# Channel attention with a folded feed-forward layer: v's second tile is loaded and transposed earlier

## The chip, the cores and the metric

The kernel runs on one core of a Trainium2 chip. A core has TensorE (PE in the profile; its weight loads are listed as PEld), VectorE (DVE), ScalarE (ACT), GpSimd (POOL) and SyncE (SP), which each run their own instructions in order and wait for one another by semaphores. Sixteen DMA engines move data between device memory and SBUF (on-chip memory with 128 partitions), and within SBUF; TensorE writes its results to PSUM banks, from which VectorE and ScalarE copy them. The metric is the time of one execution on the device, in microseconds (us); less is better.

## The reference

The inputs are q, k and v of 4 x 6080 x 256, two weights, w_in (256 x 2048) and w_out (2048 x 256), and three scalars. All is float32.

```
qn = q / (norm(q, axis=1) + 1e-6);  kn = k / (norm(k, axis=1) + 1e-6)   # norms over the 6080 rows
s  = kn^T @ qn / tau                  # 256 x 256 for each batch
a  = softmax(s, last axis)
x  = (v @ a) as 24320 rows of 256
h  = x @ w_in;  r = max(h, 0);  g = s * r * r + b
out = g @ w_out
```

## The kernel before

**Algebra.** Since x = v a and h = x w_in, the kernel multiplies a by w_in first, once for each batch. The result (`wa`, 256 x 2048, held as two halves of 128 partitions by 2048 columns) is called the folded weight, and h is then v wa. The softmax's division is done as a scaling of the rows of the folded weight by `rs`, the reciprocal of the sums of the exponentials.

**Start, batch 0.** q and k come in 13 chunks of up to 512 rows, nearly all by DMAs that POOL issues and that convert from float32 to float16 on the way (the first three tiles come as float32 from SP's and ScalarE's queues). For each chunk TensorE adds to the Gram matrix `s_ps` (line 154), while ScalarE and VectorE form squares for the norms. The last chunks' k tiles are loaded before their q tiles. Between the chunks' matmuls `keep_busy` (line 551) issues filler matmuls, whose results nobody reads: one after each of the chunks 8, 7 and 6 from the end, two after the chunks 5 and 4 from the end (`FILL`, line 549). When the norms are summed, ScalarE makes the inverse norms of k and then of q (line 277, four steps each), VectorE scales the Gram matrix (line 302), and ScalarE takes the exponentials in two halves, `eT` (line 308).

**First block.** `first_block` (line 340) makes the first 256 columns of the folded weight. For each half of the exponentials it issues two matmuls for the row sums `r_ps` (line 347) and two for the product with w_in (line 352). VectorE then takes the reciprocal (line 356), and the two halves are scaled out of PSUM in pieces of 128 columns, one half by ScalarE (line 329), the other by VectorE (line 331). Before this block TensorE transposes v's first tile (`transpose_v`, line 463: eight transposes of 128 x 128 into one PSUM bank, then one VectorE copy of 128 x 1024), and one more filler is issued (line 595).

**Main loop.** The 24320 rows go in 48 groups of 512 (the last is of 256), and each group in 16 steps of 128 columns of the hidden layer, so step s is group s // 16, column block s % 16. In each step `mm1` (line 761) makes h for one column block; ScalarE and VectorE apply relu and square; then products with w_out follow, for most groups by a scheme of seven products of half size (line 932). The remaining blocks of batch 0's folded weight (`fold_one`, line 361) are issued at steps 0, 0, 1, 1, 3, 3, 5, 5, 8, 8 right after `mm1`: first columns 256 to 512, then 512 to 768, 768 to 1024, 1024 to 1536, 1536 to 2048.

**What sets the order.** The order on every engine is the order of the calls in the program (`po` keeps it). `at_step` puts side work at fixed steps: the transposes of v's second tile at step 12 (line 692), while from the third tile on v is transposed by DMAs from SP's queue (`crossbar_v`). POOL issues its DMAs in this order: q and k, v tile 0, the five pieces of w_in (256, 256, 512, 512 and 512 columns), v tile 1, four pieces of w_out, v tile 2, two scalars.

**Buffers.** PSUM has one Gram bank (`ps_gram`), two h tiles of two banks (`ps_h`) and three banks for everything else (`ps_o`), which each new tile takes in turn. `first_block` takes its two products from one o bank and one h tile, its row sums from an o bank; `bank` (line 442) gives that. v has four SBUF buffers for tiles as loaded and three for transposed ones.

Of the kernel before, what the change touches and what calls it, by code (L numbers as in the profile page):

```python
# [9 lines left out]
FP32 = mybir.dt.float32  # L10
# [6 lines left out]
def kernel(  # L17
# [12 lines left out]
    nc = tc.nc  # L30
    P = 128

    B, N, C = q.shape
# [11 lines left out]
    CH = C // P  # L45
    FT = Dff // P
# [8 lines left out]
    def po(ins):  # L55

        tc.keep_in_program_order(ins)
        return ins

    def pool(name, bufs, **kw):  # L60
        return ctx.enter_context(tc.tile_pool(name=name, bufs=bufs, **kw))
# [19 lines left out]
    ps_gram = pool("ps_gram", 1, space=PSUM)  # L81
# [9 lines left out]
    def h_tile(name):  # L91
        return ps_h.tile([P, 2, TG], FP32, tag="h_ps", name=name)
# [19 lines left out]
    class Gram:  # L112
# [147 lines left out]
        def finish_ops(self):  # L260
# [3 lines left out]
            def inverse(a=None):  # L264

                n = C + CH if a is None else (CH, C)[a]

                def part(i):
                    if i == 0:
                        st["r", a] = sm_pool.tile([P, n], FP32, tag=f"r{a}", name=f"r{a}")  # L270
                        if a is None:
                            st["r", 1], st["r", 0] = st["r", a][:, :C], st["r", a][:, C:]
                    r = st["r", a]
                    func, kw = [(AF.Ln, dict(bias=tiny)), (AF.Exp, dict(scale=0.5)),
                                (AF.Ln, dict(bias=eps)), (AF.Exp, dict(scale=-1.0))][i]
                    sums = self.n_all if a is None else self.n_ps[a]
                    po(nc.scalar.activation(out=r, in_=r if i else sums, func=func, **kw))  # L277
                    if i == 3 and a != 1 and inv_tau != 1.0:
                        po(nc.vector.tensor_scalar_mul(
                            out=st["r", 0], in0=st["r", 0], scalar1=inv_tau))  # L280

                return [lambda i=i: part(i) for i in range(4)]

            def norms(a):
                return lambda: self.add_norms(a, last=True)
# [19 lines left out]
            def exps(j):  # L305
                if j == 0:
                    st["e"] = sm_pool.tile([P, CH, C], FP16, tag="eT", name="eT")
                po(nc.scalar.activation(  # L308
                    out=st["e"][:, j, :], in_=st["t"][:, j], func=AF.Exp,
                    scale=st["r", 0][:, j : j + 1]))  # L310
                if j == 0:
                    self.wa = apool.tile([P, CH, Dff], FP16, tag="wa16", name="wa16")
# [12 lines left out]
            def scaled(f0, n, m, wa_ps):  # L325
                dst = self.wa[:, m, ds(f0, n)]
                third = self.b == 0 and f0 == 2 * NW
                if m == third and not (self.b == 0 and NW <= f0 < 2 * NW):
                    po(nc.scalar.mul(out=dst, in_=wa_ps, mul=st["rs"][:, m : m + 1]))  # L329
                else:  # L330
                    po(nc.vector.tensor_scalar_mul(
                        out=dst, in0=wa_ps, scalar1=st["rs"][:, m : m + 1]))
# [4 lines left out]
                                        w_in16[:, j, ds(f0, n)],  # L337
                                        start=(j == 0), stop=(j == CH - 1)))

            def first_block(n):  # L340

                two = [self.bank("wa_ps", CH, C)[:, 0, :n], h_tile("wa_ps")[:, 0, :n]]
                r_ps = self.bank("r_ps", CH, C)[:, :, 0]
                for j in range(CH):
                    exps(j)
                    for ch in range(CH):
                        po(nc.tensor.matmul(r_ps[:, ch : ch + 1], st["e"][:, j, ts(ch, P)],
                                            parts16, start=(ch == 0 and j == 0),
                                            stop=(ch == CH - 1 and j == CH - 1),
                                            skip_group_check=True))  # L350
                    for m in range(CH):
                        po(nc.tensor.matmul(two[m], st["e"][:, j, ts(m, P)],
                                            w_in16[:, j, :n],
                                            start=(j == 0), stop=(j == CH - 1)))
                st["rs"] = sm_pool.tile([P, CH], FP32, tag="rs", name="rs")
                po(nc.vector.reciprocal(out=st["rs"], in_=r_ps))
                for f0 in range(0, n, P):
                    for m in range(CH):
                        scaled(f0, P, m, two[m][:, ds(f0, P)])

            def fold_one(f0, n, m):
                def f():
                    wa_ps = self.bank("wa_ps", CH, C).rearrange("p a c -> p (a c)")[:, :n]
                    fold_mm(f0, n, m, wa_ps)
                    if self.b == 0 and f0 == 2 * NW and m == 1:
                        return at_step(5, lambda: scaled(f0, n, m, wa_ps))
                    scaled(f0, n, m, wa_ps)
                return f
# [60 lines left out]
            if self.b == 0:  # L429
                blocks = [(2 * P, 2 * P), (4 * P, 2 * P), (6 * P, 2 * P), (2 * NW, NW), (3 * NW, NW)]  # L430
                folds = [fold_one(f0, n, m) for f0, n in blocks for m in range(CH)]
                return [norms(1), *inverse(1), norms(0), *inverse(0), lambda: scale(CH),
                        lambda: first_block(2 * P)] + folds

            def sums_and_halves():
                sums()
# [12 lines left out]
    def group(g):  # L449
        t0 = g * TG  # L450
        return t0, min(TG, NT - t0) // P
# [3 lines left out]
    def load_v(g):  # L455
        t0, nj = group(g)
        v16 = vpool.tile([P, TG // P, C], FP16, tag="v16", name="v16")
        po(nc.gpsimd.dma_start(  # L458
            out=v16[:, :nj, :],
            in_=v_flat[t0 : t0 + nj * P, :].rearrange("(p j) c -> p j c", j=nj)))  # L460
        v_tiles[g] = v16

    def transpose_v(g):
        _, nj = group(g)
        v16 = v_tiles.pop(g)
        vT_ps = ps_o.tile([P, CH, TG], FP16, tag="o_ps", name="vT_ps")
        for j in range(nj):
            for ch in range(CH):
                po(nc.tensor.transpose(vT_ps[:, ch, ts(j, P)], v16[:, j, ts(ch, P)], ident16))  # L469
        vT = vtpool.tile([P, CH, TG], FP16, tag="vT", name="vT")  # L470
        po(nc.vector.tensor_copy(out=vT[:, :, : nj * P], in_=vT_ps[:, :, : nj * P]))
        vT_tiles[g] = vT

    def crossbar_v(g):

        _, nj = group(g)
        v16 = v_tiles.pop(g)
        vT = vtpool.tile([P, CH, TG], FP16, tag="vT", name="vT")
        for j in range(nj):
            po(nc.sync.dma_start_transpose(out=vT[:, :, ts(j, P)], in_=v16[:, j, :]))  # L480
        vT_tiles[g] = vT
# [25 lines left out]
    for c in range(NDIRECT, len(g0.chunks) - NLATE):  # L507
        g0.load(c)
        if c == NDIRECT:
            po(nc.gpsimd.affine_select(  # L510
                out=ident16, in_=ones_id, compare_op=ALU.is_equal, fill=0.0, base=0,
# [8 lines left out]
    def load_w_in(f0, f1, co=None):  # L520
        cs = slice(0, CH) if co is None else slice(co, co + 1)
        po(nc.gpsimd.dma_start(out=w_in16[:, cs, f0:f1], in_=w_in_rows[:, cs, f0:f1]))

    load_v(0)
    load_w_in(0, 2 * P)
    load_w_in(2 * P, NW)
    load_w_in(NW, 2 * NW)
    load_w_in(2 * NW, 3 * NW)
    load_w_in(3 * NW, Dff)
    w_out_rows = moe_w_out.rearrange("(fo p) d -> p fo d", p=P)  # L530
    load_v(1)

    NPIECE = FT // 4
    w_pieces = []
# [11 lines left out]
    g0.start()  # L546
    NCH0 = len(g0.chunks)

    FILL = {-8: 1, -7: 1, -6: 1, -5: 2, -4: 2}

    def keep_busy(n):

        for _ in range(n):
            po(nc.tensor.matmul(h_tile("idle_ps")[:, 0, :], fill[:, :P], fill, start=True,
                                stop=True, skip_group_check=True))

    norms_k, *rest = g0.finish_ops()
    inverse_k, norms_q, inverse_q, scale_s, first_block, folds = (
        rest[:4], rest[4], rest[5:9], rest[9], rest[10], rest[11:])
    late = range(NCH0 - NLATE, NCH0)  # L560
    for c in range(NCH0 - NLATE):
        ops = g0.norm_ops(c)
        for j in range(g0.chunks[c][2]):
            g0.mm(c, j)
        keep_busy(FILL.get(c - NCH0, 0))
        if c == NCH0 - NLATE - 1:
# [25 lines left out]
    for f in (*inverse_q, scale_s):  # L592
        f()
    transpose_v(0)
    keep_busy(1)
    first_block()


    acc = opool.tile([P, 4, C], FP32, tag="o_sb", name="acc")
# [60 lines left out]
    def at_step(s, f):  # L660
        side.setdefault(int(s), []).append(f)
# [6 lines left out]
    for i, f in enumerate(folds):  # L668
        early.setdefault(FOLDS[i], []).append(f)
    at_step(14, lambda: po(nc.vector.tensor_scalar_mul(  # L670
        out=s_out, in0=s_bc, scalar1=1.0 / (LAM * LAM))))
# [15 lines left out]
    for g in range(NG):  # L687
        if g >= 3:
            at_step(max(g - 4, 0) * FT + 2, lambda g=g: load_v(g))
        if g >= 1:  # L690
            if g == 1:
                at_step(12, lambda g=g: transpose_v(g))
            else:
                at_step((g - 2) * FT + 6, lambda g=g: crossbar_v(g))
    LATER = {(1, 0): {1: 5, 2: 4, 3: 3}, (1, 1): {0: 6, 1: 3, 2: 3, 3: 4, 4: 4},
             (1, 2): {0: 4, 1: 1, 2: 2, 3: 2, 4: 2}, (1, 11): {2: 1, 3: 1}}
    for b in range(2, B):
# [3 lines left out]
    for b in range(1, B):  # L701
# [6 lines left out]
        n = NCH * JC  # L708
# [247 lines left out]
    for s in range(NS + FT):  # L956
        g, m = divmod(s, FT)
# [8 lines left out]
        if work:  # L966
            items, n = work[0]
# [61 lines left out]
```

## Time and profile before

| what | value |
| --- | --- |
| median of 3 runs | 714.37 us (714.33 to 714.67) |
| span of the profiled execution, first to last instruction | 712.9 us |
| time of the profiled execution outside its span | not listed |
| TensorE busy | 692.9 us, 97% |
| VectorE, ScalarE, GpSimd busy | 635.6, 547.5, 114.1 us |
| mean granted TensorE clock | 0.998 |
| time before the first TensorE matmul | 10.96 us |
| first L761 matmul (main loop begins) | 37.84 us |

The profile is of one execution. Times count from its first instruction, so the span leaves out what the device does before the first and after the last instruction; the median of the runs holds that too. In the tables of stretches the columns are the stretch in us from the span's start, its length, then for PE, PEld, DVE, ACT and POOL the busy time with the number of instructions, then the granted TensorE clock (1.00 is full speed), the DMA engines' share and the GB/s that they moved. In a timeline each line gives start, time, engine, line of the kernel, operation, output and input tiles, and the count where several follow one another; brackets hold the idle time before it and what ended that. TensorE's matmuls are pipelined, so the time of a group reaches beyond the start of the next. The lists of DMA issues give the size and the us from issue to landing. Some matmul records can be missing from a trace.

### The profile page before, as it was taken

What the parts mean: (1) busy time and instruction counts of PE and PEld (TensorE: products, weight loads), DVE (VectorE), ACT (ScalarE), POOL (GpSimd) and SP (SyncE); (2) the same over time, 40 slices, a digit from 0 to 9 for tenths busy, and PEclk for the clock granted to TensorE, in tenths of its full rate; (3) what the DMA queues carried; (4) which work ended last, traced back from release to release, by engine and by line L of the source; (5) the groups of instructions that cost most, each with busy time, mean ns of one, the idle gap of its engine ahead of it and who ended that gap; (6) DMA issues with size and microseconds to landing.
All of it is one profiled execution on the core that took longest, in us unless ns stands there. A gap on an engine that the chain in (4) does not pass through costs nothing.

```text
span 712.9 us, 17531 instructions
## 1 busy us (share of the span) xinstructions
PE 692.9 (97%) x7422; PEld 502.9 (71%) x7422; DVE 635.6 (89%) x906; ACT 547.5 (77%) x598; POOL 114.1 (16%) x192
## 2 busy tenths in 40 slices
PE   3699999999999999999999999999999999999998
PEld 2456777776677777777677777777768777777777
DVE  4889999999988989998999899998998888888886
ACT  5689877787777777778877777777876777777875
POOL 4533132201202222111010222111000000000000
PEclk9999999999999999999999999999999999999999
DMA  9999999566566878465761888737323333321202
GB/s 213 207 259 168 186 164 137 114 109 122 105 136 109 133 137 144 110 92 101 156 131 50 148 134 150 129 76 96 101 65 75 94 71 75 97 61 46 83 31 75
DMA packets 87854, 83.55 MB, mean 117 GB/s; under 512 B 56368, under 2 KB 62784, under 8 KB 87776
## 3 DMA queue, kind: packets, MB, share of 16 engines
q0 software_dynamic: 27136, 44.00, 38.9%
q1 hardware_dynamic: 60128, 37.45, 21.1%
q8 instruction: 58, 0.95, 0.6%
q10 hardware_dynamic: 512, 0.98, 0.4%
q14 instruction: 20, 0.16, 0.1%
HBM read 78.91 MB, written 24.90 MB: 146 GB/s over the span
## 4 chain that ended last, share of the span: by engine, by line
PE 95%; DMA 4%; ACT 1%; issue 0%; DVE 0%; ACTq 0%; POOLq 0%
PE h_ps L761 46%; PE o_ps L932 40%; PE s_ps L154 5%; DMA qk<-in_q_dram 2%; DMA qk<-in_k_dram 1%; PE wa_ps L394 1%; PE o_ps L836 1%; PE o_ps L808 0%; PE wa_ps L336 0%; ACT r L277 0%; PE n_ps L252 0%; ACT sq L185 0%; ACT eT L308 0%; PE vT_ps L469 0%; DVE half L229 0%
## 5 line engine op out<-in xcount | busy, mean ns | idle before, releaser
L771 ACT ACTIVATE r<-h_ps 128x1024 f16<-128x1024 f32 (+1 forms) x384 | 388.5, 1013 | 144.2 <-PE h_ps L761 140.6
L761 PE MATMUL h_ps<-vT,wa 128*128 128x512 f16 (+7 forms) x1632 | 452.1, 364 | 0.5 <-ACT wa L329 0.5
L932 PEld LDWEIGHTS <-S 128*128 128x128 f16 x2944 | 198.1, 98 | 84.3
L932 PEld LDWEIGHTS <-g 128*128 128x128 f16 x2208 | 155.0, 98 | 74.0
L784 DVE TENSOR_TENSOR g<-r 128x2048 f16<-128x2048 f16 (+2 forms) x150 | 174.4, 1163 | 10.1 <-ACT r L771 9.7
L932 PE MATMUL o_ps<-T,S 128*128 128x128 f16 x2208 | 183.1, 219 | 0.0
L761 PEld LDWEIGHTS <-wa 128*128 128x128 f16 x1632 | 136.6, 98 | 19.0 <-ACT wa L329 1.0
L932 PE MATMUL o_ps<-w_out,g 128*128 128x128 f16 x1472 | 134.2, 219 | 0.0
L782 ACT ACTIVATE g<-r 128x1024 f16<-128x1024 f16 (+1 forms) x97 | 100.3, 1034 | 0.2
L789 DVE SCALAR_TENSOR_TENSOR o_sb<-o_ps,s_out,u 128x256 f32<-128x256 f32 x138 | 66.2, 480 | 36.1 <-PE o_ps L932 34.5
L154 PE MATMUL s_ps<-qk 128*128 128x256 f16 (+1 forms) x384 | 71.0, 287 | 15.6 <-ACT qk L145 11.0
L458 POOL DMA_DIRECT2D v<-in_v_dram x48 | 31.4, 662 | 239.9 <-DMA vT<-v 192.7
L215 POOL DMA_DIRECT2D f<-f x33 | 28.8, 874 | 245.9 <-DVE f L199 197.3
L789 DVE SCALAR_TENSOR_TENSOR u<-o_ps,s_out,rowconst 128x256 f32<-128x256 f32 x138 | 65.7, 476 | 0.0
L932 PE MATMUL o_ps<-w_out,S 128*128 128x128 f16 x736 | 63.5, 219 | 0.0
L932 PE MATMUL o_ps<-N,g 128*128 128x128 f16 x736 | 63.4, 219 | 0.0
L185 ACT ACTIVATE sq<-qk 128x1024 f16<-128x1024 f16 (+2 forms) x53 | 54.5, 1041 | 4.5 <-DMA qk<-in_k_dram 1.9
L861 DVE TENSOR_TENSOR S<-S,g 128x2048 f16<-128x2048 f16 (+1 forms) x47 | 56.4, 1200 | 1.2
L859 DVE TENSOR_TENSOR S<-g 128x2048 f16<-128x2048 f16 (+1 forms) x47 | 56.0, 1192 | 0.0
L863 DVE TENSOR_TENSOR S<-g 128x2048 f16<-128x2048 f16 x46 | 55.8, 1214 | 0.0
L865 DVE TENSOR_TENSOR S<-g,S 128x2048 f16<-128x2048 f16 x46 | 55.8, 1213 | 0.0
L154 PEld LDWEIGHTS <-qk 128*128 128x128 f16 (+1 forms) x384 | 33.0, 103 | 21.2 <-ACT qk L145 11.0
(103 smaller groups left out, 334.4 us busy)
## 6 DMA issues: line engine op xcount, KB each, us to landing
out_dram<-o_sb SPq DMA_DIRECT2D x43, 512.0 KB, 3.0
v<-in_v_dram POOLq DMA_DIRECT2D x47, 256.0 KB, 5.0
qk<-in_q_dram POOLq DMA_DIRECT2D x43, 256.0 KB, 7.7
qk<-in_k_dram POOLq DMA_DIRECT2D x42, 256.0 KB, 6.4
f<-f POOLq DMA_DIRECT2D x30, 128.0 KB, 3.1
vT<-v SPq DMA_TRANSPOSE x182, 3.0
w<-in_moe_w_out_dram POOLq DMA_DIRECT2D x4, 512.0 KB, 9.9
out_dram<-o_sb SPq DMA_DIRECT2D x8, 256.0 KB, 4.1
```

The lines of the kernel that those rows point to most:

```text
L154: po(nc.tensor.matmul(self.s_ps[:, ch, :], qc[:np_, j, ts(ch, P)], kc[:np_, j, :], start=(c == 0 and j == 0 and ch == 0), stop=(c == len(s ...
L185: po(nc.scalar.activation(out=st["sq"][:np_, a, js, :], in_=(qc, kc)[a][:np_, js, :], func=AF.Square))
L761: po(nc.tensor.matmul(dst, wa[:, ci, ts(m, P)], src, start=(ci == 0), stop=(ci == CH - 1), skip_group_check=True))
L771: po(nc.scalar.activation(out=r16[:, :, i % 2, :n], in_=h_tiles.pop((g, i))[:, :, :n], func=AF.Relu))
L782: po(nc.scalar.activation(out=dst, in_=src, func=AF.Square))
L784: po(nc.vector.tensor_mul(dst, src, src))
L789: po(nc.vector.scalar_tensor_tensor(out=dst, in0=src, scalar=s_out, op0=ALU.mult, in1=add, op1=ALU.add))
L859: po(nc.vector.tensor_add(T[1], A21, A22))
L861: po(nc.vector.tensor_sub(T[2], T[1], A11))
L863: po(nc.vector.tensor_sub(T[3], A11, A21))
L865: po(nc.vector.tensor_sub(T[4], A12, T[2]))
L932: po(nc.tensor.matmul(st[name][:, j, :], a()[:, i, ts(j, P)], w[:, i, :], start=first, stop=last, skip_group_check=True))
```

## The change

Five things change.

- The DMA of v's second tile is issued right after that of the first, ahead of the five pieces of w_in.
- v's second tile is transposed on TensorE before the first block, where a filler stood; the transposes at step 12 go.
- Its copy out of PSUM is made in two halves (128 x 512 each). The first is issued on VectorE before the reciprocal, the second after the scalings of the first block.
- `first_block` takes its two products from the two banks of one h tile, and its row sums from the Gram bank.
- The fillers after the chunks 8, 7 and 6 from the end are left out; those after 5 and 4 stay.

```diff
-            def first_block(n):
-                two = [self.bank("wa_ps", CH, C)[:, 0, :n], h_tile("wa_ps")[:, 0, :n]]
-                r_ps = self.bank("r_ps", CH, C)[:, :, 0]
+            def first_block(n, between, after):
+                both = h_tile("wa_ps")
+                two = [both[:, m, :n] for m in range(CH)]
+                r_ps = ps_gram.tile([P, CH, C], FP32, tag="s_ps", name="r_ps")[:, :, 0]
                 for j in range(CH):
                     exps(j)
...
+                between()
                 st["rs"] = sm_pool.tile([P, CH], FP32, tag="rs", name="rs")
                 po(nc.vector.reciprocal(out=st["rs"], in_=r_ps))
                 for f0 in range(0, n, P):
                     for m in range(CH):
                         scaled(f0, P, m, two[m][:, ds(f0, P)])
+                after()
...
-                        lambda: first_block(2 * P)] + folds
+                        lambda *fs: first_block(2 * P, *fs)] + folds
...
-    def transpose_v(g):
+    def transpose_v(g, parts=1):
...
         vT = vtpool.tile([P, CH, TG], FP16, tag="vT", name="vT")
-        po(nc.vector.tensor_copy(out=vT[:, :, : nj * P], in_=vT_ps[:, :, : nj * P]))
         vT_tiles[g] = vT
+        def copy(part):
+            cs = slice(0, CH) if parts == 1 else slice(part, part + 1)
+            po(nc.vector.tensor_copy(out=vT[:, cs, : nj * P], in_=vT_ps[:, cs, : nj * P]))
+        if parts == 1:
+            return copy(0)
+        return [lambda i=i: copy(i) for i in range(parts)]
...
     load_v(0)
+    load_v(1)
     load_w_in(0, 2 * P)
     load_w_in(2 * P, NW)
     load_w_in(NW, 2 * NW)
     load_w_in(2 * NW, 3 * NW)
     load_w_in(3 * NW, Dff)
     w_out_rows = moe_w_out.rearrange("(fo p) d -> p fo d", p=P)
-    load_v(1)
...
-    FILL = {-8: 1, -7: 1, -6: 1, -5: 2, -4: 2}
+    FILL = {-5: 2, -4: 2}
...
     transpose_v(0)
-    keep_busy(1)
-    first_block()
+    first_block(*transpose_v(1, CH))
...
-        if g >= 1:
-            if g == 1:
-                at_step(12, lambda g=g: transpose_v(g))
-            else:
-                at_step((g - 2) * FT + 6, lambda g=g: crossbar_v(g))
+        if g >= 2:
+            at_step((g - 2) * FT + 6, lambda g=g: crossbar_v(g))
```

## The prediction

> **What bounds the kernel now.** I read the engines' totals and the chain that ended last, then TensorE's busy time by stretch, then the order of time between 28 and 42 us, which is where the change acts.
>
> ```profile
> PE 692.9 (97%) x7422; PEld 502.9 (71%) x7422; DVE 635.6 (89%) x906; ACT 547.5 (77%) x598; POOL 114.1 (16%) x192
> PE 95%; DMA 4%; ACT 1%; issue 0%; DVE 0%; ACTq 0%; POOLq 0%
> ```
>
> ```profile
> 38.00:100.00 62.00, 62.00 (x547) 42.48 (x546) 59.87 (x97) 54.25 (x64) 19.78 (x34) 1.00 1.04 200
> ```
>
> The second fence is the table by stretch (PE busy first, granted clock third from the end). TensorE is busy in all 62 of 62 us, at clock 1.00, and so in every later stretch up to 700. The end is therefore the start of the first L761 matmul, at 37.84 us, plus TensorE's work after it, plus any new hole. VectorE is busy 59.87 us there, but the waits of TensorE after 38 us list no VectorE. Before 31 us the transfers bind (205 GB/s, DMA share above 1), then a chain through ScalarE up to the exponentials.
>
> ```profile
> 35.39 0.62 PE L469 MATMUL vT_ps<-ident,v 128*128 128x128 f16 x8
> 35.82 0.47 PE L554 MATMUL idle_ps<-fill 128*128 128x512 f32 x1
> 36.52 0.20 PE L347 MATMUL r_ps<-parts,eT 128*128 128x1 f16 x2 [0.23 <-ACT eT L308]
> 36.58 0.38 PE L352 MATMUL wa_ps<-w_in,eT 128*128 128x256 f16 x2
> 36.92 0.20 PE L347 MATMUL r_ps<-parts,eT 128*128 128x1 f16 x2
> 36.98 0.38 PE L352 MATMUL wa_ps<-w_in,eT 128*128 128x256 f16 x2
> 37.84 0.60 PE L761 MATMUL h_ps<-vT,wa 128*128 128x512 f16 x2 [0.48 <-ACT wa L329]
> ...
> 35.38 0.45 PEld L469 LDWEIGHTS <-v 128*128 128x128 f16 x8 [0.39 <-DMA v<-in_v_dram]
> ```
>
> In TensorE's timeline the first tile of v is already waited for: it lands at 35.3 and its transposes start at 35.38. The first block starts at 36.52, held by the exponentials, and ends at 36.98 + 0.38 = 37.36. So there is about 1 us between the landing of v's first tile and the work that sets the end.
>
> ```profile
> 28.31 0.53 POOL L458 DMA_DIRECT2D v<-in_v_dram  x1 [0.80 <-DMA qk<-in_k_dram]
> 29.55 0.74 POOL L522 DMA_DIRECT2D w_in<-in_moe_w_in_dram  x1 [0.70 <-DMA qk<-in_q_dram]
> 30.75 2.13 POOL L522 DMA_DIRECT2D w_in<-in_moe_w_in_dram  x3 [0.47 <-DMA qk<-in_k_dram]
> 33.15 0.70 POOL L522 DMA_DIRECT2D w_in<-in_moe_w_in_dram  x1 [0.27 <-DMA qk<-in_q_dram]
> 33.85 0.57 POOL L458 DMA_DIRECT2D v<-in_v_dram  x1
> ```
>
> ```profile
> v<-in_v_dram POOLq DMA_DIRECT2D x1, 256.0 KB, 7.0
> ...
> w_in<-in_moe_w_in_dram POOLq DMA_DIRECT2D x1, 128.0 KB, 6.4
> ...
> w_in<-in_moe_w_in_dram POOLq DMA_DIRECT2D x1, 128.0 KB, 7.2
> ...
> w_in<-in_moe_w_in_dram POOLq DMA_DIRECT2D x1, 256.0 KB, 7.4
> ...
> q8 instruction: 1, 0.02, 2.0%
> ```
>
> POOL's issues in order of time, then those issues' times to landing, asked one by one. Issue plus time gives: v tile 0 at 28.31 + 7.0 = 35.31; w_in columns 0 to 256 at 29.55 + 6.4 = 35.95; columns 256 to 512 at 30.75 + 7.2 = 37.95; columns 512 to 1024 at about 31.46 + 7.4 = 38.86 (the group of three split evenly). The reader is to see that the queue is in order and full, so whatever is put in front delays everything behind it by its own transfer.
>
> **The change part by part.**
>
> *Second v tile ahead of w_in.* It is one issue of 0.53 us on POOL, moved past five of 0.70 to 0.74. Nothing moves on SP. POOL itself runs over 6 us ahead of the landings, so its order costs nothing; the transfers do. 256 KB at the 204 to 206 GB/s of these microseconds take 1.27 us. So v tile 1 lands at 35.31 + 1.27 = 36.58 and the five pieces of w_in 1.27 us later each: 37.22, 39.22, 40.13 and so on. What follows on POOL (w_out, v tile 2) keeps its place and date.
>
> *Transposes before the first block.* Eight transposes occupy TensorE for 0.45 us (the chain has them at 47.58 as "0.45 PE vT_ps L469 x8"). TensorE works in order: behind the landing at 36.58 they run from 36.65 to 37.10. Queued behind them are the row sums and the first block, which started at 36.52. The first block's products then wait for w_in, to 37.22. From there two products (0.22), two sums (0.06), two products (0.22) and the drain (about 0.16, the 0.38 of a pair less its 0.22) end at 37.88, against 37.36. Both exponentials are done by 36.9, so nothing else holds them. Delay: 0.52, call it 0.54 with the semaphore hop seen at 36.47 to 36.52. ScalarE, VectorE and the first L761 wait for this end; L761 goes from 37.84 to 38.38.
>
> *The next two pieces.* The first fold of columns 256 to 512 ran at 38.29; it would run at 38.83, but its w_in lands at 39.22: 0.41 more with the hop. Columns 512 to 1024 were wanted at 39.16, now at 39.16 + 0.95 = 40.11, and land at 40.13: nothing more. The pieces for 41.76 and 43.91 landed at 40.1 and 41.4 and stay ahead by 1 us and more. Delay in all: 0.95.
>
> *The copy out of PSUM in two halves.* One copy of 0.68 us at 48.06 goes, two of 128x512 come. The trace has none of that shape: the 0.68 of double the size bounds it from above and half of it, 0.34, from below; I take 0.41, as for the half-width additions just before. The first half stands ahead of the reciprocal on VectorE, from 37.27 to 37.68; the row sums end at about 37.64, so the reciprocal is held 0.04 (0 to 0.3 by the bounds) and ends at 37.86, still before the first block's product at 37.88. The second follows the scalings and fits before the next fold, where VectorE had 0.69 idle. The copy saved at 48 us hides already behind TensorE: 0.
>
> *Transposes gone from step 12.* 0.45 us off TensorE's solid stretch: a full gain of 0.45.
>
> *Three fillers at 20, 22.5 and 25 us, and the one at 35.82, left out.* Each was 0.47 us inside waits for q tiles (1.18, 1.27 and 1.18 us) and, the last, for the exponentials. Covered by those waits: 0 in time. What they did to the clock is the second rival.
>
> *PSUM places.* The first block takes one h tile in place of one and an o bank, the row sums the Gram's bank, free since the scaling at 36.14: 0.
>
> Sum: 0.54 + 0.41 - 0.45 = +0.50 us. Bounds: the second piece of w_in came 2.00 us after the first, where its 128 KB take 0.64 at 205 GB/s. The excess of 1.36 stands beside one packet of the instruction queue, which took 2.0% of 16 engines in a window of 3 us, 0.96 us of one engine. If it falls behind these pieces, 0.41 goes: +0.09. If it falls on v tile 1, that lands at 37.94, transposes end at 38.45 and the first block at 39.1, but w_in's 39.22 then costs nothing extra: +1.3. If on the first piece of w_in, landing at 38.58: 1.88 - 0.45 = +1.43. I take the middle because the packet comes with TensorE's program (at 35.89 it was near the filler), which the change lets wait at just that place until 36.6; it then meets the second piece as before.
>
> The sum is against the profiled execution, whose span is 712.9; no other time of that execution is listed. The median of the runs, 714.37, lies 1.5 us outside the span, which I carry over: 714.37 + 0.50 = 714.9.
>
> **The rivals.**
>
> *Hidden anyway.* If v and w_in land sooner than in order, only the transposes are left ahead of the block: they end at 37.10 or earlier, against 36.52 to 36.9, about 0.4, and the gain is 0.45. Time 714.2 to 714.4; at best, with no delay at all, 713.9. For it: w_in's first need is for two of its 16 column blocks only. Against: 99% busy transfers.
>
> *The clock drops.* This ends slower.
>
> ```profile
> 23.62:27.04 3.42, 1.56 (x12) 1.15 (x13) 3.18 (x8) 2.65 (x3) 1.59 (x4) 1.00 1.13 211
> 27.04:30.45 3.41, 3.38 (x16) 2.04 (x14) 2.15 (x5) 2.11 (x2) 1.75 (x3) 0.50 1.13 205
> 33.86:37.28 3.42, 3.09 (x44) 1.99 (x42) 2.06 (x6) 2.81 (x9) 2.68 (x4) 1.00 1.28 200
> ```
>
> After a stretch with 1.56 of 3.42 us busy the next had clock 0.50; after the full one it was 1.00 again. In 33.86 to 37.28 TensorE was busy 3.09; without the filler and with the wait for v it is about 1.42 + 0.62 + 0.62 = 2.66, above 1.56, so I take no drop: 0. If it drops at 37.28, the stretch up to 40.69 runs at half speed. The work that would be done in it, about 2.3 us of full rate, shrinks to about 1.4 because of the new waits: +0.9 on top of 0.5, 715.8. Where the drop falls on a solid stretch it costs 3.41 / 2 = 1.7: 716.6. It decides from the point where the busy time that counts falls to about 1.6 in such a stretch. The missing fillers before 26 us may bring a drop earlier, but the four that stay fill 27 to 31.4, where it came back.
>
> A rule speaks against the change here. The Trainium skill, "TensorE: Matmul & The Clock Gate", Part 4, says that transposes do not count as busy time for the clock as other matmuls do. By it the window would hold 1.42, under the 1.56 that lost the clock, and the sum would be +1.4 instead of +0.5; no row here tells, since in the one window with transposes other work was enough.
>
> *The instruction packet hits v or w_in's first piece.* +1.3 to +1.43, 715.7 to 715.8, as worked out above.
>
> **How the numbers follow.** Forecast (+0.1 to +1.0) 0.50; hidden anyway 0.12; clock 0.16; packet 0.15; something unseen 0.07. A measurement of this kernel can tell 0.2%, 1.43 us, from no change. So within 0.2%: 0.50 + 0.12, half of the packet's (0.08) and 0.02 of the clock's: 0.72. Slower: 0.14 + 0.07 + 0.04 = 0.25. Faster: 0.03, since TensorE has only 0.45 to give. Range: 714.1, below the forecast's low end of 714.46 and into the hidden case, to 716.2, between the clock's two prices; about 0.1 is left out at each end.
>
> **What would show it.** In the changed profile: v tile 1 landing near 36.6 with TensorE waiting for it; the first L352 waiting for w_in to about 37.2; the first L761 at 38.4 and not 37.84; a hole before the first L336 of up to 0.5; no transposes at 47.6; solid TensorE work after 41 with about 0.45 us less of it; clock 1.00 after 31. It is wrong if L761 starts by 38.0, if a stretch after 33.9 has clock 0.50, or if TensorE shows holes after 42.

## The result and the profile after

The changed kernel took 717.38 us (median of 5 runs, 716.74 to 718.43) against 714.40 us (714.33 to 715.45) for the kernel before. The ratio is 1.0043, with a 95% interval of 1.0032 to 1.0055: slower by 3.0 us. The forecast was 714.9, with 714.1 to 716.2 as its range.

The profiled execution's span went from 712.9 to 715.4 us. First the page's totals and the chain's window from 34 us, where each line gives start, length and what it was.

```profile
PE 693.1 (97%) x7418; PEld 502.3 (70%) x7418; DVE 635.8 (89%) x907; ACT 547.6 (77%) x598; POOL 114.6 (16%) x192
```

```profile
29.65 8.24 DMA v<-in_v_dram
37.89 0.05 issue
37.94 0.62 PE vT_ps L472 x8
...
39.55 0.38 ACT wa L329
39.93 0.04 issue
39.98 1.03 PE h_ps L767 x2
```

TensorE's busy time is the same, 693.1 us against 692.9, though four fillers are gone and the transposes only moved: part of the work ran slower. The chain no longer passes through the exponentials but through the transfer of v's second tile, which took 8.24 us from its issue and landed at 37.89 us. Now TensorE's timeline around the first block:

```profile
35.43 0.62 PE L472 MATMUL vT_ps<-ident,v 128*128 128x128 f16 x8
37.94 0.62 PE L472 MATMUL vT_ps<-ident,v 128*128 128x128 f16 x8 [1.89 <-DMA v<-in_v_dram]
38.40 0.19 PE L348 MATMUL r_ps<-parts,eT 128*128 128x1 f16 x2
38.45 0.59 PE L353 MATMUL wa_ps<-w_in,eT 128*128 128x256 f16 x2
38.83 0.24 PE L348 MATMUL r_ps<-parts,eT 128*128 128x1 f16 x2
38.93 0.59 PE L353 MATMUL wa_ps<-w_in,eT 128*128 128x256 f16 x2
39.98 1.03 PE L767 MATMUL h_ps<-vT,wa 128*128 128x512 f16 x2 [0.46 <-ACT wa L329]
40.80 1.06 PE L336 MATMUL wa_ps<-w_in,eT 128*128 128x256 f16 x4
41.66 0.71 PE L767 MATMUL h_ps<-vT,wa 128*128 128x512 f16 x2
42.20 0.60 PE L336 MATMUL wa_ps<-w_in,eT 128*128 128x256 f16 x4
```

TensorE stands 1.89 us for v. The first block's row sums start at 38.40 and not at 36.52. The pair of L353 takes 0.59 where it took 0.38, the main loop's first pair 1.03 where it took 0.60, the first four folds 1.06 against 0.60. Only at 42.20 are four folds back at 0.60. The table by stretch says why (length, busy times, and granted clock third from the end):

```profile
35.06:38.47 3.41, 1.50 (x23) 1.05 (x21) 1.35 (x3) 1.80 (x7) 1.22 (x3) 1.00 1.28 199
38.47:41.88 3.41, 2.95 (x17) 1.47 (x15) 1.63 (x5) 1.14 (x3) 2.85 (x5) 0.50 1.21 260
41.88:45.30 3.42, 3.42 (x21) 1.92 (x20) 3.16 (x7) 2.41 (x4) 1.34 (x3) 1.00 1.05 362
```

The stretch with the stand was busy 1.50 us, and the next ran at half clock. A third thing shows in the two engines that scale the first block, here ScalarE's and then VectorE's timeline:

```profile
39.55 0.37 ACT L329 ACTIVATE wa<-wa_ps,rs 128x128 f16<-128x128 f32 x1 [2.56 <-PE wa_ps L353]
40.34 0.37 ACT L329 ACTIVATE wa<-wa_ps,rs 128x128 f16<-128x128 f32 x1 [0.42 <-DVE wa L331]
```

```profile
39.95 0.35 DVE L331 TENSOR_SCALAR wa<-wa_ps,rs 128x128 f16<-128x128 f32 x1 [0.68 <-ACT wa L329]
40.74 0.35 DVE L331 TENSOR_SCALAR wa<-wa_ps,rs 128x128 f16<-128x128 f32 x1 [0.44 <-ACT wa L329]
```

Before, ScalarE did its two from 37.42 and VectorE its two from 37.44, side by side. Now each waits for the other, since both read one PSUM tile.

**Where the 2.6 us of the spans went.** The row sums start 1.88 us later. From there to the first main matmul it is 1.58 us against 1.32, 0.26 more. From there to the third and fourth of the early folds it is 2.22 (39.98 to 42.20) against 1.32, 0.90 more. Together 3.04; without the transposes at step 12, 0.45 less; so 2.59, and the spans differ by 2.60 (715.45 and 712.85 before rounding). The medians differ by 2.98; the 0.4 beyond the spans lies outside them and in the spread of the runs, and is not traced here.

A fourth thing costs nothing in this trace but matters below. POOL issues the sixth v tile's load at 50.49 us, where the kernel before did it at 59.47. Kernel before, then after:

```profile
49.95 0.53 POOL L137 DMA_DIRECT2D qk<-in_q_dram  x1 [0.27 <-DMA v<-in_v_dram]
59.47 0.53 POOL L458 DMA_DIRECT2D v<-in_v_dram  x1 [8.99 <-DVE g L784]
```

```profile
50.49 0.54 POOL L461 DMA_DIRECT2D v<-in_v_dram  x1
51.01 0.55 POOL L137 DMA_DIRECT2D qk<-in_k_dram  x1
51.53 0.56 POOL L137 DMA_DIRECT2D qk<-in_q_dram  x1
52.68 0.54 POOL L137 DMA_DIRECT2D qk<-in_k_dram  x1 [0.60 <-DMA v<-in_v_dram]
53.70 0.53 POOL L137 DMA_DIRECT2D qk<-in_q_dram  x1 [0.48 <-DMA qk<-in_k_dram]
```

### The profile page after: what moved, and what is told of

It reads as the page before. It is cut to its first block, busy times and chain, and to the rows that moved or that the text cites. A ratio compares the mean times of both kernels' runs of the same rounds, so it can differ in the third digit from the quotient of the medians.

```text
span 715.4 us, 17523 instructions
## 1 busy us (share of the span) xinstructions
PE 693.1 (97%) x7418; PEld 502.3 (70%) x7418; DVE 635.8 (89%) x907; ACT 547.6 (77%) x598; POOL 114.6 (16%) x192
## 3 DMA queue, kind: packets, MB, share of 16 engines
q0 software_dynamic: 27136, 44.00, 38.6%
## 4 chain that ended last, share of the span: by engine, by line
PE 94%; DMA 4%; POOL 1%; issue 0%; ACT 0%; DVE 0%; POOLq 0%
PE h_ps L767 46%; PE o_ps L938 40%; PE s_ps L154 4%; DMA qk<-in_k_dram 2%; DMA qk<-in_q_dram 1%; PE wa_ps L397 1%; DMA v<-in_v_dram 1%; PE o_ps L842 1%; POOL qk L137 1%; PE o_ps L814 0%; PE wa_ps L336 0%; PE wa_ps L353 0%; PE vT_ps L472 0%; PE rc_ps L619 0%; ACT wa L329 0%
```

## The experiments

The theory after this profile: v's second tile lands late because a packet of TensorE's own instructions holds one DMA engine just then; TensorE stands (waits idle) for it, and the stand costs the clock. The runs are called e1 to e16; in front of each result stands its edit, against the kernel before, the changed kernel or the run just told of, and what was expected. Rivals: the three missing fillers cost the clock; the shared PSUM tile is the loss; the transfer order costs by itself, whatever stands for v. The medians below are each against the kernel before in the same session on the same chip; the intervals of the ratios are about 0.1% wide to either side, so that steps of 0.2 us between two of them are read from the traces and not from the medians.

### Fillers, from both sides

```diff
-    FILL = {-5: 2, -4: 2}
+    FILL = {-8: 1, -7: 1, -6: 1, -5: 2, -4: 2}
```

> The changed kernel with the three early fillers put back. Late-tile theory (the second v tile lands near 37.9 us, TensorE stands until then, and this stand also loses the clock): nothing changes where it counts, first main matmul near 40.0 us, a half-clock stretch behind it, time 717 to 717.7 us. Filler theory (the missing fillers let the clock fall): the clock stays at 1.00 after 31 us, first main matmul near 39.5, time 716.3 us or less.

e1: 717.50 against 714.29, ratio 1.0048 (1.0035 to 1.0060). The first main matmul came at 40.12, and half clock from 37.08 to 43.90. The other side, the kernel before without those three fillers:

```diff
-    FILL = {-8: 1, -7: 1, -6: 1, -5: 2, -4: 2}
+    FILL = {-5: 2, -4: 2}
```

> The kernel before with only the three early fillers left out. Late-tile theory: same as before, 714.3 to 714.9 us, first main matmul at 37.8 to 38.0 us; the clock may fall earlier than 27 us but is back by about 31 us. Filler theory: a stretch at half clock behind 33 us and 715.3 us or more.

e6: 714.42 against 714.43, ratio 1.0000 (0.9990 to 1.0009). The first main matmul came at 37.72 and the clock was 1.00 from 30.9 us on, though it had fallen at 20.7 already. The three fillers cost and bring nothing; that rival is out, and that term of the forecast, 0, held.

### The clock

```diff
     transpose_v(0)
+    keep_busy(6)
     first_block(*transpose_v(1, CH))
```

> The changed kernel with six fillers (1.3 us of TensorE) between the transposes of the first and of the second v tile, inside the stand for the second. Clock theory: the stretch before 38.5 us is then busy enough, the clock is 1.00 from 31 us to the end, and the time falls by 0.9 to 1.7 us, to 715.7 to 716.5 us; the first main matmul comes at about 39.6 (the wait for v itself stays). If the clock is not a cause: 717.4 us as without them.

e2: 716.48 against 714.29, ratio 1.0037 (1.0025 to 1.0050), 0.9 us under the change. In its trace the clock was 1.00 from 30.3 us to the end of the loop, and a pair of L353 took 0.38 again; but that execution took 718.72 us, its loads came 1.5 us late, and v's second tile landed 1.24 us behind the first, so that TensorE did not stand for it. The trace of e15 below, with the same six fillers, has the stand: v's second tile lands at 37.55, and the clock is 1.00 from 30.36 us on.

```profile
37.59 0.62 PE L472 MATMUL vT_ps<-ident,v 128*128 128x128 f16 x8 [0.37 <-DMA v<-in_v_dram]
38.10 0.38 PE L353 MATMUL wa_ps<-w_in,eT 128*128 128x256 f16 x2
```

So the clock is a cause, of about 0.9 us: from the row sums to the third and fourth of the early folds it takes 2.77 us in e15 (38.05 to 40.82) against 3.80 in the change (38.40 to 42.20).

### Load order and transposes apart

```diff
-    first_block(*transpose_v(1, CH))
+    keep_busy(1)
+    first_block(lambda: None, lambda: None)
...
+        if g == 1:
+            at_step(12, lambda g=g: transpose_v(g))
```

> The changed kernel with the second v tile still loaded ahead of w_in, but transposed at step 12 as before, and with the filler before the first block. Late-tile theory: no stand on v; the first block waits for w_in alone, first products near 37.3 us, first main matmul near 38.4, clock 1.00 after 31 us, time 715.0 to 715.6 us. If the transfer order itself is what costs (w_in late by 1.3 us or more): first products near 38.5 us, time 716.3 us or more.

e4: 717.78 against 714.29, ratio 1.0049 (1.0035 to 1.0063), and the runs lie between 716.04 and 718.77. This is a miss for the theory that the stand on v is the loss: nothing stands on v here, and yet it is no faster. The trace of it (its execution took 716.04) has the stand in another place:

```profile
36.26 0.20 PE L348 MATMUL r_ps<-parts,eT 128*128 128x1 f16 x2 [0.33 <-ACT eT L308]
37.98 0.38 PE L353 MATMUL wa_ps<-w_in,eT 128*128 128x256 f16 x2 [1.51 <-DMA w_in<-in_moe_w_in_dram]
```

The first piece of w_in lands at 37.98, and not at 37.22 as forecast. The next one moves the transposes of the changed kernel into the wait for the scaling:

```diff
-    first_block(*transpose_v(1, CH))
+    keep_busy(1)
+    turned = []
+    first_block(lambda: turned.extend(transpose_v(1, CH)), lambda: [f() for f in turned])
```

> The changed kernel with the second v tile transposed after the first block's products, where TensorE waits for the scaling, and the filler before the first block kept. Late-tile theory: the first block no longer waits for v; the transposes begin near 37.9 us, in or just behind the hole, and cost at most 0.5 us there; first main matmul near 38.4 to 38.7, clock 1.00 after 31 us, 714.9 to 715.7 us. If the order of the transfers is what costs, 716.3 us or more.

e7: 716.99 against 714.43, ratio 1.0034 (1.0022 to 1.0047). Again TensorE stood 1.49 us for w_in, to 37.82, and the clock was 0.50 from 37.42. Both say: after the load order the first block waits to about 38 us, for one tile or the other. Is the rest of e4 the clock? With eight fillers in its wait instead of one:

```diff
-    keep_busy(1)
+    keep_busy(8)
     first_block(lambda: None, lambda: None)
```

> The changed kernel with the second v tile loaded ahead of w_in but transposed at step 12, and eight fillers (1.7 us) before the first block, inside the wait for w_in. Clock theory: with the wait filled the clock is 1.00 after 31 us in nearly every run, so the runs scatter by under 0.6 us in place of 2.7, and what is left is the price of the order alone: first products near 37.95, first main matmul near 39.1, 715.9 to 716.3 us. If the clock is not what scatters them: 716 to 718.8 us as without the fillers.

e12: 716.18 against 714.43, ratio 1.0025 (1.0015 to 1.0035), and the nine runs lie between 715.94 and 716.36, a scatter of 0.42 us in place of 2.73. This fits the clock as what scatters e4's runs, but does not show it: no late execution of e4 was profiled, and the mean granted clock was 0.990 in the run of 718.77 but 0.995 both at 716.04 and at 717.82. With the wait filled, the order costs 1.75 us; the packet and the shared tile, below, are in that. Putting the first 256 columns of w_in back ahead of v gives the piece that matters:

```diff
     load_v(0)
-    load_v(1)
     load_w_in(0, 2 * P)
+    load_v(1)
```

> The changed kernel with the first 256 columns of w_in loaded ahead of the second v tile, which is transposed at step 12, and the filler before the first block. If the late first piece of w_in is the whole loss: first products at 36.5 us, first main matmul at 37.8, then up to 0.9 us of wait for the next columns (landing near 39.2), clock 1.00 after 31 us, time 714.6 to 715.6 us. If the order of the later pieces costs as much as the first: 716 us or more.

e10 (transposes at step 12, one filler before the block): 715.39 against 714.43, ratio 1.0016 (1.0007 to 1.0024). The first products start at 36.69 and the first main matmul at 37.96; the next two pieces of w_in are waited for by 0.19 and 0.24 us. So of the order's 1.75 us the late first piece is 0.6 to 0.8 (716.18 less 715.39 is 0.79; in the traces the third and fourth folds start at 40.80 in e12 and at 40.18 in e10), and the rest is the later pieces and the shared tile.

### The instruction packet

The queue of instructions moved one packet of 16 KB at 35.86 us in the changed kernel; it is in the list of DMA queues for 35.8 to 36.9 us:

```profile
q8 instruction: 1, 0.02, 5.5%
```

5.5% of 16 engines over 1.1 us is 0.97 us of one engine, and v's second tile was moving then. That the packet is TensorE's own is seen from its date in the runs below, and fits the count: 58 such packets in the whole kernel before, and 2 x 7422 matmuls and weight loads, 256 to a packet. To shift the packet, 16 instructions that TensorE runs early are left out; the Gram sum then lacks the second chunk.

```diff
-        for j in range(g0.chunks[c][2]):
+        for j in range(g0.chunks[c][2] if c != 1 else 0):
             g0.mm(c, j)
```

> The changed kernel without the Gram matmuls of batch 0's second chunk (left out: 8 matmuls with their weight loads, so 16 instructions fewer on TensorE before 17 us; the Gram sum lacks that chunk). Packet theory (one 16 KB packet of TensorE's instructions at 35.86 us holds one DMA engine for 0.97 us in the middle of the second v tile): the packet comes 16 instructions later in the program, behind the transposes of the first v tile, and the second v tile lands 0.8 to 1.3 us sooner, near 36.6 to 37.0 us. If the second tile is late for another reason (order of the queue, the issue): it lands at 37.8 us again.

```profile
36.54 0.62 PE L472 MATMUL vT_ps<-ident,v 128*128 128x128 f16 x8 [0.61 <-DMA v<-in_v_dram]
37.00 0.19 PE L348 MATMUL r_ps<-parts,eT 128*128 128x1 f16 x2
38.60 0.38 PE L353 MATMUL wa_ps<-w_in,eT 128*128 128x256 f16 x2 [1.42 <-DMA w_in<-in_moe_w_in_dram]
```

e5: the packet now came between 36.4 and 37.5 us. V's second tile was there at 36.5, 1.40 us sooner and where the forecast had it (36.58). But the first piece of w_in, moving when the packet came, was late instead: 38.6. The time was 717.62 against 714.43, ratio 1.0045 (1.0032 to 1.0059). So the lateness moved with the packet, from the one transfer to the next. With 32 instructions fewer (the second and third chunks left out of the Gram sum) it comes behind both:

```diff
-        for j in range(g0.chunks[c][2]):
+        for j in range(g0.chunks[c][2] if c not in (1, 2) else 0):
```

> The changed kernel without the Gram matmuls of batch 0's second and third chunks (left out: 16 matmuls with their weight loads, 32 instructions of TensorE before 20 us; the Gram sum lacks both chunks). Packet theory: the instruction packet comes after the second v tile and the first piece of w_in; v lands near 36.6, w_in's first piece near 37.2, the first main matmul starts near 38.4, and the time is 714.6 to 715.3 us if the clock holds, which is what was forecast for the change. Order theory (the queue is late by more than the second v tile's own 1.27 us whatever the packet does): w_in's first piece lands at 37.9 or later, time 716.5 us or more.

```profile
36.75 0.62 PE L472 MATMUL vT_ps<-ident,v 128*128 128x128 f16 x8 [0.60 <-ACT eT L308]
37.20 0.19 PE L348 MATMUL r_ps<-parts,eT 128*128 128x1 f16 x2
37.42 0.38 PE L353 MATMUL wa_ps<-w_in,eT 128*128 128x256 f16 x2
...
38.56 0.78 PE L767 MATMUL h_ps<-vT,wa 128*128 128x512 f16 x2 [0.48 <-ACT wa L329]
...
65.53 0.59 PE L767 MATMUL h_ps<-vT,wa 128*128 128x512 f16 x2 [1.38 <-DMA vT<-v]
```

e9: the first part is the forecast nearly to the number: v landing at 36.70 (29.68 plus 7.0; the bracket names the exponentials, which the transposes do not read), w_in at 37.4, the first main matmul at 38.56 (38.4 forecast), clock 1.00. And yet 716.70 against 714.43, ratio 1.0034 (1.0021 to 1.0046), another miss: a new wait of 1.38 us has come, at 65.53, for the DMA transposes of v's third tile. In all, v's second tile landed 2.46 to 2.64 us behind the first in the seven traces in which the packet began 0.43 to 0.59 us behind that landing, and 1.22 to 1.23 us behind it in the four in which the packet began 1.2 us behind it or later. The kernel before shows the packet's price by itself, when 32 tiny instructions bring it forward:

```diff
+        if c == NCH0 - 8:
+            for _ in range(16):
+                po(nc.tensor.matmul(h_tile("tiny_ps")[:, 0, :1], ones16, ones16[:, 0:1],
+                                    start=True, stop=True, skip_group_check=True))
```

> The kernel before with 16 tiny matmuls more (128 x 1 outputs, 32 instructions) behind the Gram chunk 8 from the end, where TensorE waits for q; they take under 1 us there. Packet theory: the packet comes about 1 us sooner and falls on the first v tile or the first piece of w_in, which land up to 1 us later; the first block starts up to 0.5 us later, 714.5 to 715.0 us. If the packet holds nothing up: 714.4 us.

e11: 715.32 against 714.43, ratio 1.0017 (1.0008 to 1.0026). The packet came further forward than expected, between 30.5 and 31.6 us, and the q tiles behind it were late: the first block's row sums started at 37.25 instead of 36.52, behind the exponentials, and the first main matmul at 38.57 instead of 37.84. So 16 KB of instructions cost 0.9 us here (0.73 in the trace, up to the first main matmul), where the transfers behind them are waited for.

### The wait for the third tile's transposes

V's third tile is transposed by four DMAs. The third and fourth, issued between 52.3 and 54.3 us, land 12.3 us later in the changed kernel and 5.1 in the kernel before (median us in the last column; before, then after), the last one at 65.8 and at 58.9 us:

```profile
vT<-v SPq DMA_TRANSPOSE x2, 5.1
```

```profile
vT<-v SPq DMA_TRANSPOSE x2, 12.3
```

The suspects are the five loads that POOL issues 8 to 9 us sooner. In the kernel before they waited for a buffer of v that comes free only with these transposes (the last landed at 58.91, the load went out at 59.47, and the same 0.55 to 0.56 us lie between the two in the nine other traces in which this load was not early); in the changed kernel the second tile's buffer is free early. Three buffers instead of four hold the loads back in the run e9:

```diff
-    vpool = pool("vpool", 4)
+    vpool = pool("vpool", 3)
```

> The run with the packet out of the way (Gram matmuls of the second and third chunks left out), and v's tiles as loaded in three buffers instead of four, so that the sixth tile's load must wait for the third tile's DMA transposes, as in the kernel before. Early-loads theory: the loads behind it go back to about 59 us, the transposes land near 59, the 1.4 us wait at 64 us goes, 715.0 to 715.4 us. If the wait is not from these loads: 716.7 us as with four buffers.

e13: the sixth tile's load went out at 59.70, TensorE's waits list no transposes, and the time was 715.08 against 714.34, ratio 1.0013 (1.0004 to 1.0022): 1.6 us less than e9. In the kernel before, with nothing else changed:

```diff
-    vpool = pool("vpool", 4)
+    vpool = pool("vpool", 5)
```

> The kernel before with five buffers for v's tiles as loaded instead of four, and nothing else. Early-loads theory: the sixth tile's load and four q and k loads go out near 50.5 us instead of 59.5, the DMA transposes of the third tile land near 65.4, and TensorE waits for them at 64 us for about 1.3 us: 715.5 to 716.0 us. If the loads do no harm: 714.4 us.

```profile
51.36 0.53 POOL L458 DMA_DIRECT2D v<-in_v_dram  x1
```

```profile
PE h_ps L761 <- DMA vT<-v: 3.0, 1, 3.0
```

```profile
vT<-v SPq DMA_TRANSPOSE x2, 11.6
```

e14: these are POOL's issue, TensorE's wait and the landing, here of the third tile's second and third transposes. 716.33 against 714.34, ratio 1.0024 (1.0014 to 1.0034). One buffer more makes this kernel 2.0 us slower; the profiled execution took 720.37 us, so its 3.0 us of wait are above what the median has. So the early loads delay the transposes: with them the wait comes, without them it goes. With three buffers where only the clock was repaired:

```diff
-    vpool = pool("vpool", 4)
+    vpool = pool("vpool", 3)
...
+    keep_busy(6)
     first_block(*transpose_v(1, CH))
```

> The changed kernel with six fillers in the wait for v's second tile and three buffers for v's tiles as loaded. With the clock held and no wait for the third tile's transposes, what is left is the late first block alone: first products near 38.4, first main matmul near 39.6, less the 0.45 us of the eight transposes: 715.8 to 716.2 us, against 716.5 with four buffers. If the transposes' landing is no floor here: 716.5 us.

e15: 715.90 against 714.34, ratio 1.0024 (1.0014 to 1.0034), 0.6 less than with four buffers. That fits the landing of the transposes as a floor for e2, whose trace waits 1.3 us for them, but the step is within the intervals of the two ratios.

### The shared PSUM tile

```diff
-                both = h_tile("wa_ps")
-                two = [both[:, m, :n] for m in range(CH)]
+                two = [self.bank("wa_ps", CH, C)[:, 0, :n], h_tile("wa_ps")[:, 0, :n]]
```

> The changed kernel with the two products of the first block in two separate PSUM tiles again (one o bank, one h tile). Shared-tile theory: ScalarE and VectorE scale at the same time again instead of in turn, the second scaling of each ends 0.5 to 0.7 us sooner, and the time falls by 0.2 to 0.7 us, to 716.7 to 717.2 us. Late-tile and clock theory: in a half-clock stretch the first main matmul takes as long as the second scaling waits, so nothing is gained, 717.2 to 717.6 us.

e3: 717.18 against 714.29, ratio 1.0043 (1.0031 to 1.0056). ScalarE and VectorE scale side by side again, two in 0.62 and two in 0.61 us, but the half clock behind 38.7 us hides it. The other way round, the kernel before with the changed PSUM places alone:

```diff
-                two = [self.bank("wa_ps", CH, C)[:, 0, :n], h_tile("wa_ps")[:, 0, :n]]
-                r_ps = self.bank("r_ps", CH, C)[:, :, 0]
+                both = h_tile("wa_ps")
+                two = [both[:, m, :n] for m in range(CH)]
+                r_ps = ps_gram.tile([P, CH, C], FP32, tag="s_ps", name="r_ps")[:, :, 0]
```

> The kernel before with only the PSUM places of the first block changed (both products in one h tile, row sums in the Gram's bank). Shared-tile theory: ScalarE and VectorE scale in turn; the main loop's second matmul and the next column block wait for that, 0.2 to 0.7 us: 714.6 to 715.1 us. If the tool that orders the accesses does not make them take turns here: 714.4 us.

e8: 714.63 against 714.43, ratio 1.0004 (0.9995 to 1.0012). The interval holds no change; the trace has the first pair of main matmuls at 0.77 us against 0.60, a wait of 0.17, which is the size of the difference. And with everything else out of the way, as e13 (two Gram chunks left out, three buffers) with the products in separate tiles:

> As e13, with the two products of the first block in separate PSUM tiles. Everything that was found is then taken away but the second v tile's own transfer time: first main matmul near 38.4, 0.2 us less than e13 from the scaling at the same time, 714.8 to 715.2 us; the forecast for the change was 714.9. A value above 715.6 us would mean that a further cost is still hidden.

```profile
38.35 0.78 PE L766 MATMUL h_ps<-vT,wa 128*128 128x512 f16 x2 [0.48 <-ACT wa L329]
39.37 0.61 PE L336 MATMUL wa_ps<-w_in,eT 128*128 128x256 f16 x4 [0.24 <-DMA w_in<-in_moe_w_in_dram]
```

e16: 715.00 against 714.34, ratio 1.0008 (0.9999 to 1.0017). What is left, 0.7 us, is the second v tile's own transfer ahead of w_in, less the 0.45 us gained. The packet came at 37.3 us here and fell on w_in's second piece, which is the case that the forecast had taken as its middle: first main matmul at 38.35 (38.38 forecast), a wait of 0.24 for the second piece (0.41), and 0.7 us (0.50). No version here was faster than the kernel before.

## Why the prediction was wrong

**What held.** TensorE binds the rest of the program: the delay at the end is the delay of the main loop less 0.45 us for the eight transposes, to 0.01 us. The second tile's own transfer time is 1.27 us (37.22 forecast for w_in's first piece; 37.38 in e9, 37.17 in e16), and the sum of +0.50 made from it came out as 0.7 in e16, whose interval holds it. The copies in halves were 0.42 us (0.41 taken), the reciprocal followed at once, the early fillers were worth 0, POOL's issues themselves cost nothing.

**The step that failed.** "I take the middle because the packet comes with TensorE's program (at 35.89 it was near the filler), which the change lets wait at just that place until 36.6; it then meets the second piece as before." The packet came at 35.86 us, just before TensorE began to stand (36.05), and met v's second tile, which landed at 37.89 in place of 36.58. The stand did not hold it back: it came 2.1 us before TensorE's next instruction ran (37.94). The forecast had priced this case, at +1.3 us, and put 0.15 on it together with the case of w_in's first piece; it was the case in seven of the eight traces of the change's load order in which nothing was moved to shift the packet (e2's late execution is the eighth). Worse, the forecast moved the packet and the order of the pieces as two separate risks. In fact what comes behind the packet is late too (w_in's first piece at 38.22 in the change), so that taking the second tile out of TensorE's way (e4, e7) only laid bare the first piece of w_in at 37.8 to 38.0. Before, this piece had landed as the packet began (35.98 and 35.89), and the second piece, which the packet delayed, landed at 37.91 and was first used at 38.29.

**The second.** "In 33.86 to 37.28 TensorE was busy 3.09; without the filler and with the wait for v it is about 1.42 + 0.62 + 0.62 = 2.66, above 1.56, so I take no drop: 0." The drop was put on a case of its own, with 0.16. It followed from the first failure: with the stand 1.3 us longer the stretch held 1.50 us, and the clock fell. The forecast also took the stretch where the kernel before had it; in the changed kernel's profile it lay 1.2 us later (35.06 to 38.47). Filling the stand gives 0.9 us back (e2). Its working, 0.9 for a drop at the start of the loop, was right in size; that the two cases come together, +1.3 and +0.9 and 0.26 at the scaling, was not seen, and their sum lies outside the range.

**The third.** "PSUM places ... 0": two engines that read different banks of one tile take turns. 0.17 us in the trace of e8.

**The fourth, without effect in the change.** "Transposes gone from step 12. ... a full gain of 0.45" and "What follows on POOL ... keeps its place and date". The early release of v's buffer sends five loads 9 us ahead, the third tile's DMA transposes land 7 us later, and a main loop less than 1.85 us behind that of the kernel before would have waited for them (they end the wait at 65.53 in e9; the kernel before starts that group at 64.13, and the change is 0.45 faster up to there). The change's own loop was late enough to hide that; repairs of its start ran into it (1.38 us in e9, 0.3 in e7), until the buffers were cut to three.

**The rule on transposes.** The Trainium skill, "TensorE: Matmul & The Clock Gate", Part 4, has it that transposes do not count as busy time for the clock in the way that other matmuls do. Two stretches tell: that of the kernel before from 23.62 us, with 1.56 us busy and no transposes, behind which the clock fell, and one in e13. Below is e13's stretch, and then the transposes alone in it:

```profile
35.02:38.43 3.41, 2.28 (x25) 1.47 (x25) 2.30 (x6) 1.81 (x7) 2.29 (x4) 1.00 1.30 200
```

```profile
35.02:38.43 3.41, 1.24 (x16) 0.90 (x16) 1.00 1.30 200
```

Without its 16 transposes this stretch held 1.04 us, well under the 1.56 that lost the clock, and the clock was 1.00 in the stretch behind it. So here they counted, at least in part. How much is not settled, and the busy time of the table is a rough measure of what counts: the change's stretch with 1.50 us, 1.15 of it transposes, lost the clock, and so did one in e1 with 2.07 us, 0.62 of it transposes and much of the rest matmuls of one column, while in the kernel before one with 1.63 us, all of wide matmuls, kept it.

**What stays open.** That the sixth tile's load is tied to the third tile's transposes was read from the traces and tested by the number of buffers. The program fits it, since the kernel before hands the third tile to its DMA transposes at step 6 and the second tile to TensorE only at step 12; how the buffers are dealt out was not looked up. Why one packet delays v by 1.3 us, 0.3 more than its own 0.97, was not settled. Nor was why it delayed nothing in two executions that were late as a whole (718.72 us in e2, where v's second tile landed 1.24 us behind the first with the packet beside it, and 720.37 in e14, where w_in's first two pieces landed 0.71 and 0.66 us apart).

## What to carry to other kernels

Where the transfer queue is full, write down which transfers are in flight at the moment that matters, each with its landing and its first use, and count a packet of instructions among them: a change of order gives the slack of one to another, and the piece with the least slack then sets the time. Rivals that share a cause (here a longer stand and a lost clock) belong in one sum, not in two. Freeing a buffer earlier also moves the loads that waited for it, so look up whom these loads will meet.

## What was not expected of the hardware

- One 16 KB packet of instructions for TensorE takes 0.97 us of one DMA engine, and in most traces here the transfer that was moving landed 1.0 to 1.5 us later than without it. Its date follows the number of TensorE's instructions: 16 fewer moved it from about 35.8 to 36.5 us, 32 more to 30.6. In the kernel before that was worth 0.9 us.
- The third and fourth DMA transposes of v's third tile (128 x 256 each) took 5.1 us to land when the q, k and v loads were held back and 12.3 us beside five of them.
- The clock's stretches of 3.41 us lie differently in each execution (its changes were seen at 16.80 in the kernel before, 14.58 in the changed one). The runs of e4, with a stand of 1.5 us, lay between 716.0 and 718.8 us, and those of e12, with the stand filled, between 715.9 and 716.4; that the clock makes this difference is argued, not shown.
